# Transposing q and k of batches 2 to 7 by the DMA crossbar instead of by TensorE and VectorE, in a fused attention and feed-forward kernel

One core of a Trainium2 chip (trn2) runs the kernel. The metric is the device time of one execution in microseconds (us). PE is TensorE, DVE VectorE, ACT ScalarE, POOL GpSimd, SP SyncE.

## The reference

Attention over 8 batches, 8 heads, 576 positions, head size 64: a full attention on sums of four positions ("down", 144 of them) plus a local attention (distance under 4). The result, 4608 tokens of 512, goes through a feed-forward layer with 2048 hidden units. Cut:

```python
out_d     = sm_attn(q_d, k_d, v_d)           # q_d, k_d, v_d: means of four positions
out_up    = np.repeat(out_d, 4, axis=2)
scores    = np.where(abs(pos_i - pos_j) < 4, scale * q @ k.T, -1e9)
out_local = softmax(scores) @ v
x = (out_up + out_local)  ->  (4608, 512)
y = gelu(x @ w_in) @ w_out
```

## The kernel before

PE works through nine blocks `c` of 512 tokens. M1 (`x @ w_in`, 64 matmuls) of block c is followed by M2 (`@ w_out`, 64 matmuls), and into M2 the attention of batch c+1 is woven. From batch 2 on, PE transposes q and k of the next batch inside M1, so that scores can be taken at the start of M2. The parts that matter here:

```python
    def t_in(b, p, which):                      # one head pair, q or k
        nat = nat6(ld[b % 2]["qn" if which == "q" else "kn"])
        tr = ppool.tile([128, 1024], F16, tag="tr", name=f"tr_{which}")
        for c in range(NCK):                    # NCK = 6 pieces of CH = 96 positions
            nc.tensor.transpose(tr[:, CH * c:CH * c + CH], nat[:, c, 2 * p:2 * p + 2, :], I128[0:CH, 0:CH])
        if which == "q":
            nc.vector.tensor_copy(out=qT[:, p, :], in_=tr[:, 0:S])
            ...                                 # sums of four into qd, two adds on POOL
        else:
            for hh in range(2):                 # k goes into kz, zero-padded per head of the pair
                nc.vector.tensor_copy(out=kz[r, p, hh, :], in_=tr[r, 0:S])
            ...                                 # sums of four into kdz, on DVE

    # m2(c), at the last matmul of a 128-token tile (four to a block):
                    osb = wpool.tile([128, 512], F32, tag="osb", bufs=2, name="out_sb")
                    nc.scalar.copy(out=osb, in_=ps)
                    nc.sync.dma_start(out=out[r0:r0 + 128, :], in_=osb)

    for c in range(NCH):                        # b = c + 1
        ...
        elif b < B:
            v_down(b)                           # sums of four of v, on POOL, 5.2 us
            for p in range(NP):                 # NP = 4 head pairs
                f1(6 if p == 0 else 7)          # so many matmuls of M1
                t_in(b, p, "q")
                f1(7)
                t_in(b, p, "k")
            k_lo()
        f1()
        ...
            attn(b, f2, 6, 9, 9)                # attention among the matmuls of M2
        f2()
        if b + 1 < B:
            run(load_qk(b + 1))                 # POOL issues the loads
            run(load_v(b + 1))
```

The softmax here doesn't subtract the row's maximum and nothing guards it: scores larger than these inputs give would overflow.

## Time and profile before

| | before |
|---|---|
| time, us | 350.44 median of 3 (350.15 to 350.55) |
| span in the profile / PE busy / PE idle, us | 348.4 / 339.0 / 9.4 |
| one batch period, us | 36.22, all of it PE busy |
| DVE, ACT, POOL | 53%, 55%, 52% |

PE idle is the span less PE's busy time.

### The profile page before, as it was taken

How to read it: one execution, taken by the hardware profiler on the slowest of the kernel's cores; microseconds unless marked ns; L12 is line 12 of the kernel's file. 1: busy time of each engine (PE TensorE's matmuls, PEld its weight loads, DVE VectorE, ACT ScalarE, POOL GpSimd, SP SyncE). 2: the span in 40 equal slices, each digit the busy share in tenths (PEclk: the TensorE clock that was granted, in tenths of full speed). 3: DMA queues.
4: the chain of work that ended last, by engine and by line, in shares of the span. 5: the costliest groups of instructions: out<-in, count | busy, mean ns of one | idle time of the engine just before them, and what ended most of it. 6: DMA issues, size and time to landing. Idle time of an engine off the chain costs nothing.

```text
span 348.4 us, 7162 instructions
## 1 busy us (share of the span) xinstructions
PE 339.0 (97%) x2976; PEld 193.9 (56%) x2976; DVE 184.5 (53%) x338; ACT 192.8 (55%) x360; POOL 180.4 (52%) x243
## 2 busy tenths in 40 slices
PE   8898998999999999999999999999999999999996
PEld 4773455655665566555655575556655664444444
DVE  7793645747574857386747665676558470000000
ACT  3664465645764577357746764566556755614620
POOL 8957649633977298628963797369652000000000
PEclk9999999999999999999999999999999999999999
DMA  6999999920999099908990599129940001011002
GB/s 87 165 205 144 185 164 110 182 75 0 98 159 146 2 77 152 176 0 59 154 171 23 36 148 178 41 18 150 159 79 0 32 33 59 2 60 60 0 34 89
DMA packets 126543, 32.31 MB, mean 93 GB/s; under 512 B 109616, under 2 KB 122032, under 8 KB 126512
## 3 DMA queue, kind: packets, MB, share of 16 engines
q0 software_dynamic: 121184, 22.43, 82.2%
q1 hardware_dynamic: 5328, 9.44, 7.6%
q8 instruction: 23, 0.38, 0.4%
q14 instruction: 8, 0.07, 0.1%
HBM read 44.83 MB, written 9.44 MB: 156 GB/s over the span
## 4 chain that ended last, share of the span: by engine, by line
PE 88%; DMA 6%; DVE 2%; POOL 2%; issue 1%; ACT 0%; POOLq 0%
PE m_ps L224 35%; PE m_ps L200 33%; PE sc L348 4%; DMA w_in_sb<-in_moe_w_in_dram 3%; PE av L403 2%; PE tr_o L441 2%; DMA q_nat<-in_q_dram 2%; PE tr_k L237 2%; PE tr_q L237 2%; DMA k_nat<-in_k_dram 1%; DVE kz L272 1%; PE av L397 1%; PE sc L353 1%; PE m_ps L215 1%; PE av L395 1%; DVE kdz L275 1%
## 5 line engine op out<-in xcount | busy, mean ns | idle before, releaser
L200 PE MATMUL m_ps<-xT,w_in_sb 128*128 128x512 f16 x568 | 133.3, 379 | 0.5 <-ACT gT L195 0.5
L224 PE MATMUL m_ps<-w_out_sb,gT 128*128 128x512 f16 x560 | 130.3, 379 | 0.0
L203 ACT ACTIVATE gT<-m_ps 128x512 f16<-128x512 f32 x142 | 84.8, 597 | 56.7 <-PE m_ps L200 56.7
L200 PEld LDWEIGHTS <-w_in_sb 128*128 128x128 f16 x568 | 52.1, 97 | 54.7 <-issue 0.8
L224 PEld LDWEIGHTS <-gT 128*128 128x128 f16 x560 | 51.9, 98 | 54.6
L228 ACT COPY out_sb<-m_ps 128x512 f32<-128x512 f32 x35 | 20.6, 589 | 42.8 <-PE m_ps L224 37.8
L243 POOL TENSOR_TENSOR q_t<-qT 128x288 f32<-128x288 f16 x24 | 16.0, 667 | 52.0 <-DVE qT L240 37.8
L104 POOL DMA_DIRECT2D q_nat<-in_q_dram x42 | 32.6, 789 | 8.1 <-DMA w_out_sb<-in_moe_w_out_dram 5.7
L252 DVE TENSOR_REDUCE kdz<-kz 64x144 f16<-64x576 f16 x48 | 35.9, 747 | 1.5
L445 DVE TENSOR_TENSOR xT<-tr_o,xd 128x576 f16<-128x576 f16 x28 | 21.2, 758 | 26.9 <-ACT xd L444 26.9
L104 POOL DMA_DIRECT2D k_nat<-in_k_dram x42 | 32.2, 778 | 6.3 <-DMA w_in_sb<-in_moe_w_in_dram 3.5
L418 DVE TENSOR_TENSOR nall<-av,rr 128x896 f16<-128x896 f32 x29 | 31.7, 1091 | 1.0
L248 DVE COPY kz<-tr_k 64x576 f16<-64x576 f16 x48 | 21.9, 455 | 18.2 <-PE tr_k L237 17.5
L381 DVE TENSOR_TENSOR e<-e,band 128x1152 f16<-128x1152 f16 x28 | 21.0, 751 | 17.6 <-ACT e L375 17.6
L219 DVE COPY out_sa<-m_ps 128x256 f32<-128x256 f32 x2 | 0.8, 424 | 54.9 <-PE m_ps L215 54.9
L116 POOL DMA_DIRECT2D v_win<-in_v_dram x30 | 26.6, 912 | 0.0
L348 PE MATMUL sc<-qT,kz 128*128 128x112 f16 (+1 forms) x320 | 25.6, 214 | 0.0
L373 ACT ACTIVATE e<-sc 128x680 f16<-128x680 f32 x32 | 23.4, 732 | 2.0 <-PE sc L348 2.0
L348 PEld LDWEIGHTS <-kz 128*128 128x128 f16 x320 | 21.6, 97 | 0.9
L311 POOL TENSOR_TENSOR v_t<-v_grp 128x1024 f32<-128x1024 f16 x6 | 12.7, 2118 | 17.0 <-DMA v_grp<-in_v_dram 17.0
L444 ACT COPY xd<-tr_o 128x144 f16<-128x144 f16 x28 | 7.7, 276 | 22.0 <-PE tr_o L441 22.0
L375 ACT ACTIVATE e<-sc 128x472 f16<-128x472 f32 x32 | 18.2, 569 | 0.0
(168 smaller groups left out, 407.6 us busy)
## 6 DMA issues: line engine op xcount, KB each, us to landing
out_dram<-out_sb SPq DMA_DIRECT2D x35, 256.0 KB, 3.2
v_win<-in_v_dram POOLq DMA_DIRECT2D x40, 128.0 KB, 9.6
q_nat<-in_q_dram POOLq DMA_DIRECT2D x42, 96.0 KB, 3.7
k_nat<-in_k_dram POOLq DMA_DIRECT2D x42, 96.0 KB, 4.2
v_grp<-in_v_dram POOLq DMA_DIRECT2D x6, 512.0 KB, 8.8
w_in_sb<-in_moe_w_in_dram POOLq DMA_DIRECT2D x4, 512.0 KB, 8.1
w_out_sb<-in_moe_w_out_dram POOLq DMA_DIRECT2D x4, 512.0 KB, 9.4
v_lo<-in_v_dram POOLq DMA_DIRECT2D x6, 64.0 KB, 8.8
```

What stands on the lines that cost most here:

```text
L104: nc.gpsimd.dma_start(out=nat6(ld[b % 2][nm])[:, c, :, :], in_=src[b, :, CH * c:CH * c + CH, :].rearrange("h s d -> s h d"))
L116: nc.gpsimd.dma_start(out=L["vw"][:, j, :, 0:64], in_=v[b, :, W0[j]:W0[j] + 128, :].rearrange("h s d -> s h d"))
L200: nc.tensor.matmul(out=ps, lhsT=w_in_sb[:, fc, 128 * j:128 * j + 128], rhs=xT[:, fc, 512 * c:512 * c + 512], start=(fc == 0), stop=(fc == 3))
L203: nc.scalar.activation(out=g[:, j, :], in_=ps, func=ACTF.Gelu)
L224: nc.tensor.matmul(out=ps, lhsT=g[:, j, 128 * t:128 * t + 128], rhs=w_out_sb[:, j, :], start=(j == 0), stop=(j == NJ - 1))
L248: nc.vector.tensor_copy(out=kz[r, p, hh, :], in_=tr[r, 0:S])
L252: nc.vector.tensor_reduce(out=kdz[r, p, hh, :], in_=kz[r, p, hh, :].rearrange("p (g r) -> p g r", r=4), axis=AX.X, op=ALU.add)
L348: nc.tensor.matmul(out=dst, lhsT=kz[:, p, hh, W0[j]:W0[j] + 128], rhs=qT[:, p, Q0[j]:Q0[j] + QW[j]], start=(b > 0), stop=True)
L373: nc.scalar.activation(out=e2[:, :, 0:340], in_=sc2[:, :, 0:340], func=ACTF.Exp, scale=0.125)
L381: nc.vector.tensor_tensor(out=e2, in0=e2, in1=band.unsqueeze(1).broadcast_to([128, 2, S]), op=ALU.mult)
L418: nc.vector.tensor_tensor(out=nall.rearrange("p j a c -> p a j c"), in0=av4[:, :, :, 0:64], in1=rr.unsqueeze(3).broadcast_to([128, 2, 7, 6 ...
L445: nc.vector.tensor_tensor(out=xT[:, p, S * b:S * b + S].rearrange("p (g r) -> p g r", r=4), in0=tr[:, 0:S].rearrange("p (g r) -> p g r", r=4),
```

## The change

The intent is to free PE of 8 groups of six transposes per batch (and DVE of 12 copies), by letting SP issue twelve crossbar DMA transposes per batch. They write the operands in their final form. For that, the natural k is loaded with gaps of zeros, so that one 96x1024 transpose yields the zero-padded `kz`. The operands are double-buffered (`qTs`, `kzs`), to be filled a phase ahead; to pay for the space, the natural q and k have one buffer instead of two. ACT issues the outputs, since SP's queue now holds the transposes. The order of POOL changes: sums and v_down of batch b, then loads of batch b+1. Core of the diff:

```diff
-    qT = cpool.tile([128, NP, S], F16, tag="qT", name="qT")
+    qTs = [cpool.tile([128, NP, S], F16, tag=f"qT{i}", name="qT") for i in range(2)]
-    kz = cpool.tile([128, NP, 2, S], F16, tag="kz", name="kz")
+    kzs = [cpool.tile([128, NP, 2, S], F16, tag=f"kz{i}", name="kz") for i in range(2)]
...
+                if nm == "kn" and b > 1:           # two half pieces, with gaps of zeros
+                    for hh in range(2):
+                        nc.gpsimd.dma_start(
+                            out=pad(nat[nm])[:, c, :, 192 * hh:192 * hh + 64],
+                            in_=i.rearrange("(a g) s d -> g s a d", g=2)[hh])
...
+    def turn_qk(b):
+        for c in range(NCK):
+            cs = slice(CH * c, CH * c + CH)
+            nc.sync.dma_start_transpose(
+                out=kzs[b % 2].rearrange("p a g s -> p (a g) s")[:, :, cs],
+                in_=pad(nat["kn"])[:, c, :, :].rearrange("p a x -> p (a x)"))
+            nc.sync.dma_start_transpose(
+                out=qTs[b % 2][:, :, cs],
+                in_=nat6(nat["qn"])[:, c, :, :].rearrange("p h d -> p (h d)"))
...
-                    nc.sync.dma_start(out=out[r0:r0 + 128, :], in_=osb)
+                    nc.scalar.dma_start(out=out[r0:r0 + 128, :], in_=osb)
...
         elif b < B:
+            sums(b)                                # 4 on DVE (k), 4 x 2 on POOL (q)
+            k_lo()
             v_down(b)
-            for p in range(NP): ... t_in(b, p, "q") ... t_in(b, p, "k")
-            k_lo()
+            if b + 1 < B:
+                load_qk(b + 1)
+                turn_qk(b + 1)
+                run(load_v(b + 1))
```

More of the change, by code (lines that the diff above doesn't have):

```diff
@@ L64 @@
         ld.append({
-            "qn": ipool.tile([CH, 4096], F16, tag="qn", name="q_nat"),
-            "kn": ipool.tile([CH, 4096], F16, tag="kn", name="k_nat"),
             "vw": ipool.tile([128, 5, H, 65], F16, tag="vw", name="v_win"),
@@ L73 @@
         })
+    nat = {"qn": cpool.tile([CH, 4096], F16, tag="qn", name="q_nat"),
+           "kn": cpool.tile([CH, 6144], F16, tag="kn", name="k_nat")}
+    regr = wpool.tile([CH, 2, 4096], F16, tag="gT", bufs=2, name="regr")
     Gb = cpool.tile([128, 240], F16, tag="Gb", name="Gb")
@@ L80 @@
     zt = cpool.tile([128, 512], F16, tag="zt", name="zt")
-    e_t = [cpool.tile([128, 2 * S + 8], F16, tag=f"e{i}", name="e") for i in range(4)]
-    e_t0 = e_t
+    e_t = [cpool.tile([128, 2 * S + 8], F16, tag=f"e{i}", name="e") for i in range(3)]
     turn = [0]
@@ L97, in nat8, with pad @@
     def nat8(t):
-        return t[0:72, :].rearrange("p (h r d) -> p h r d", h=H, r=8)
+        return t[0:72, 0:4096].rearrange("p (h r d) -> p h r d", h=H, r=8)
+    def pad(t):
+        return t.rearrange("p (c a x) -> p c a x", c=NCK, a=NP)
     def load_qk(b):
-        for nm, src in (("qn", q), ("kn", k)):
-            for c in range(NCK):
-                nc.gpsimd.dma_start(
-                    out=nat6(ld[b % 2][nm])[:, c, :, :],
-                    in_=src[b, :, CH * c:CH * c + CH, :].rearrange("h s d -> s h d"))
-                yield
+        for c in range(NCK):
+            for nm, src in (("kn", k), ("qn", q)):
+                i = src[b, :, CH * c:CH * c + CH, :]
+                if nm == "kn" and b > 1:
[3 more added lines that the diff above has]
+                            in_=i.rearrange("(a g) s d -> g s a d", g=2)[hh])
+                else:
+                    nc.gpsimd.dma_start(out=nat6(nat[nm])[:, c, :, :], in_=i.rearrange("h s d -> s h d"))
+    def turn_qk(b):
+        for c in range(NCK):
+            cs = slice(CH * c, CH * c + CH)
[5 more added lines that the diff above has]
+                in_=nat6(nat["qn"])[:, c, :, :].rearrange("p h d -> p (h d)"))
     def load_v(b):
@@ L126, in load_qk8 @@
             nc.gpsimd.dma_start(
-                out=nat8(ld[b][nm])[:, h0:h1, :, :].rearrange("p h r d -> p h (r d)"),
+                out=nat8(nat[nm])[:, h0:h1, :, :].rearrange("p h r d -> p h (r d)"),
                 in_=src[b, h0:h1].rearrange("h (p r) d -> p h (r d)", r=8))
@@ L145 @@
         nc.vector.memset(ld[i]["vls"][:, 64:65], 4.0)
-    for i in range(4):
+    for i in range(3):
         nc.vector.memset(e_t[i][:, 2 * S:2 * S + 8], 1.0)
@@ L177 @@
                                     fill=0.0, base=3, channel_multiplier=4)
-    nc.vector.memset(kz.rearrange("p a b s -> p (a b s)").bitcast(F32), 0.0)
+    nc.vector.memset(kzs[0].rearrange("p a b s -> p (a b s)").bitcast(F32), 0.0)
     nc.vector.memset(KL.bitcast(F32), 0.0)
@@ L228, in m2, with sums @@
                     nc.scalar.copy(out=osb, in_=ps)
-                    nc.sync.dma_start(out=out[r0:r0 + 128, :], in_=osb)
+                    nc.scalar.dma_start(out=out[r0:r0 + 128, :], in_=osb)
                 yield
-    def t_in(b, p, which):
-        nat = nat6(ld[b % 2]["qn" if which == "q" else "kn"])
-        tr = ppool.tile([128, 1024], F16, tag="tr", name=f"tr_{which}")
-        for c in range(NCK):
-            nc.tensor.transpose(tr[:, CH * c:CH * c + CH], nat[:, c, 2 * p:2 * p + 2, :],
-                                I128[0:CH, 0:CH])
-        if which == "q":
-            nc.vector.tensor_copy(out=qT[:, p, :], in_=tr[:, 0:S])
-            qg = qT[:, p, :].rearrange("p (g r) -> p g r", r=4)
+    def sums(b):
+        for p in range(NP):
+            with nc.allow_low_precision(reason="sums of four, kept in fp16 as before"):
+                nc.vector.tensor_reduce(out=kdz[:, p, :, :],
+                                        in_=kzs[b % 2][:, p, :, :].rearrange("p a (g r) -> p a g r", r=4),
+                                        axis=AX.X, op=ALU.add)
+            qg = qTs[b % 2][:, p, :].rearrange("p (g r) -> p g r", r=4)
             t2 = wpool.tile([128, Sd, 2], F32, tag="qt2", bufs=2, name="q_t2")
@@ L244, in t_in @@
             nc.gpsimd.tensor_tensor(out=qd[:, p, :], in0=t2[:, :, 0], in1=t2[:, :, 1], op=ALU.add)
-        else:
-            for hh in range(2):
-                r = slice(64 * hh, 64 * hh + 64)
-                nc.vector.tensor_copy(out=kz[r, p, hh, :], in_=tr[r, 0:S])
-            for hh in range(2):
-                r = slice(64 * hh, 64 * hh + 64)
-                with nc.allow_low_precision(reason="sums of four, kept in fp16 as before"):
-                    nc.vector.tensor_reduce(out=kdz[r, p, hh, :],
-                                            in_=kz[r, p, hh, :].rearrange("p (g r) -> p g r", r=4),
-                                            axis=AX.X, op=ALU.add)
     def t_in_g(b, p, which):
-        nat = nat6(ld[b]["qn" if which == "q" else "kn"])
+        nt = nat6(nat["qn" if which == "q" else "kn"])
         trf = ppool.tile([128, 512], F32, tag="tr", name=f"tg_{which}")
@@ L260, in t_in_g @@
         for c in range(NCK):
-            nc.tensor.transpose(tr[:, CH * c:CH * c + CH], nat[:, c, 2 * p:2 * p + 2, :],
+            nc.tensor.transpose(tr[:, CH * c:CH * c + CH], nt[:, c, 2 * p:2 * p + 2, :],
                                 I128[0:CH, 0:CH])
         for c in range(NCK):
-            nc.tensor.matmul(out=trf[:, 288 + 24 * c:312 + 24 * c], lhsT=nat[:, c, 2 * p:2 * p + 2, :],
+            nc.tensor.matmul(out=trf[:, 288 + 24 * c:312 + 24 * c], lhsT=nt[:, c, 2 * p:2 * p + 2, :],
                              rhs=Gb[0:CH, 112:136], start=True, stop=True)
         if which == "q":
-            nc.vector.tensor_copy(out=qT[:, p, :], in_=tr[:, 0:S])
+            nc.vector.tensor_copy(out=qTs[b][:, p, :], in_=tr[:, 0:S])
             nc.vector.tensor_copy(out=qd[:, p, :], in_=trf[:, 288:432])
@@ L271, in t_in_g @@
                 r = slice(64 * hh, 64 * hh + 64)
-                nc.vector.tensor_copy(out=kz[r, p, hh, :], in_=tr[r, 0:S])
+                nc.vector.tensor_copy(out=kzs[b][r, p, hh, :], in_=tr[r, 0:S])
             for hh in range(2):
@@ L347, in local @@
                 nc.tensor.matmul(out=dst, lhsT=I128, rhs=nb[:, x:x + QW[j]], start=True, stop=False)
-            nc.tensor.matmul(out=dst, lhsT=kz[:, p, hh, W0[j]:W0[j] + 128],
-                             rhs=qT[:, p, Q0[j]:Q0[j] + QW[j]], start=(b > 0), stop=True)
+            nc.tensor.matmul(out=dst, lhsT=kzs[b % 2][:, p, hh, W0[j]:W0[j] + 128],
+                             rhs=qTs[b % 2][:, p, Q0[j]:Q0[j] + QW[j]], start=(b > 0), stop=True)
         for hh in range(2):
@@ L360, in scores_mm @@
                 local(sC[:, o + Q0[j]:o + Q0[j] + QW[j]], hh, j)
-        e = e_t[p % 3] if b else e_t0[p]
+        e = e_t[p % 3]
         ed = wpool.tile([128, 2, Sd], F16, tag="ed", bufs=4, name="ed")
@@ L537 @@
             n2 = "kn" if nm[1] == "k" else "qn"
-            dst = ld[1][n2][0:72, :].rearrange("p (r h d) -> p r h d", r=8, h=H)
+            dst = regr[0:72, int(nm[1] == "q"), :].rearrange("p (r h d) -> p r h d", r=8, h=H)
             nc.vector.tensor_copy(out=dst[:, :, 2 * p:2 * p + 2, :],
-                                  in_=nat8(L0[n2])[:, 2 * p:2 * p + 2, :, :].rearrange("p h r d -> p r h d"))
+                                  in_=nat8(nat[n2])[:, 2 * p:2 * p + 2, :, :].rearrange("p h r d -> p r h d"))
         elif nm[:2] in ("Tk", "Tq"):
             n2 = "kn" if nm[1] == "k" else "qn"
-            src = ld[1][n2][0:72, :].rearrange("p (r h d) -> p r h d", r=8, h=H)[:, :, 2 * p:2 * p + 2, :]
+            src = regr[0:72, int(nm[1] == "q"), :].rearrange("p (r h d) -> p r h d", r=8, h=H)
+            src = src[:, :, 2 * p:2 * p + 2, :]
             trf = banks(arg)[0][0]
@@ L556 @@
             if nm[1] == "Z":
-                cp(out=kz[r, p, hh, :].rearrange("p (t r) -> p t r", r=8), in_=tin["k", p][0][r])
+                cp(out=kzs[0][r, p, hh, :].rearrange("p (t r) -> p t r", r=8), in_=tin["k", p][0][r])
             else:
@@ L560 @@
         elif nm[:2] == "QT":
-            cp(out=qT[:, p, :].rearrange("p (t r) -> p t r", r=8), in_=tin["q", p][0])
+            cp(out=qTs[0][:, p, :].rearrange("p (t r) -> p t r", r=8), in_=tin["q", p][0])
         elif nm[:2] == "QD":
@@ L593 @@
             cp(out=xT[:, p, 512:576], in_=half[1][:, 0:64])
-    run(load_qk(1))
+    load_qk(1)
     for f in range(4):
@@ L598 @@
     load_vw(1)
+    nc.vector.memset(kzs[1].rearrange("p a b s -> p (a b s)").bitcast(F32), 0.0)
     nc.vector.tensor_copy(out=band[:, 0:116], in_=B0[:, 0:116])
@@ L614 @@
             k_lo()
+            nc.gpsimd.memset(pad(nat["kn"])[:, :, :, 64:192], 0.0)
+            load_qk(2)
+            turn_qk(2)
+            run(load_v(2))
         elif b < B:
+            sums(b)
+            k_lo()
             v_down(b)
-            for p in range(NP):
-                f1(6 if p == 0 else 7)
-                t_in(b, p, "q")
-                f1(7)
-                t_in(b, p, "k")
-            k_lo()
+            if b + 1 < B:
+                load_qk(b + 1)
+                turn_qk(b + 1)
+                run(load_v(b + 1))
         f1()
@@ L631 @@
         f2()
-        if b + 1 < B:
-            run(load_qk(b + 1))
-            run(load_v(b + 1))
 _INS = ['q', 'k', 'v', 'moe_w_in', 'moe_w_out']
```

## The prediction

> **What bounds the kernel now.** I read the page first, then PE's waits, then PE's timeline in a batch that repeats, then the DMA view and the POOL timeline. The page says which engine is full:
>
> ```profile
> span 348.4 us, 7162 instructions
> PE 339.0 (97%) x2976; PEld 193.9 (56%) x2976; DVE 184.5 (53%) x338; ACT 192.8 (55%) x360; POOL 180.4 (52%) x243
> ...
> PEclk9999999999999999999999999999999999999999
> DMA  6999999920999099908990599129940001011002
> ```
>
> PE is at 97%, the other compute engines near half, and the granted clock is full throughout. DMA is near full in somewhat more than half of the slices and empty between: it works in bursts, one per batch. A busy PE may still be a waiting PE, so I ask for PE's waits over the whole run:
>
> ```profile
> PE m_ps L547 <- DVE q_nat L539: 1.5, 1, 1.5
> PE spin L490 <- DVE dum L136: 1.3, 1, 1.3
> PE av L395 <- DVE v_lm L289: 0.8, 1, 0.8
> PE tg_k L261 <- DMA k_nat<-in_k_dram: 0.6, 2, 0.4
> ...
> PE av L397 <- DVE v_lm L291: 0.2, 1, 0.2
> ```
>
> These are all the large ones, and all lie before 57 us. From 73 us on PE never waits: batches 2 to 7 repeat with a period of 36.22 us (the first scores of batches start at 198.13 and 234.35), and in those 36.22 us PE is busy for 36.22. So PE's own instruction stream sets the end, and an instruction taken off PE there is worth exactly the slot that it occupies. The slot is read from PE's timeline:
>
> ```profile
> 180.96 1.46 PE L200 MATMUL m_ps<-xT,w_in_sb 128*128 128x512 f16 x6
> 182.25 0.42 PE L237 MATMUL tr_q<-I,q_nat 96*128 96x96 f16 x6
> 182.51 1.68 PE L200 MATMUL m_ps<-xT,w_in_sb 128*128 128x512 f16 x7
> 184.02 0.42 PE L237 MATMUL tr_k<-I,k_nat 96*128 96x96 f16 x6
> 184.28 1.68 PE L200 MATMUL m_ps<-xT,w_in_sb 128*128 128x512 f16 x7
> ```
>
> Durations overlap, so starts are to be read: six transposes hold PE from 182.25 to 182.51, 0.26 us, though one is listed with 206 ns.
>
> **What the Trainium skill says.** (1) "VectorE: DVE Perf Modes", section "The three transpose paths", gives 390 ns for a 128x128 two-byte transpose on TensorE and 1309 ns for the DMA crossbar. This trace does not agree for PE: in a stream one 96x96 piece costs 0.26/6 = 43 ns. So little is to be won per transpose, and the crossbar must win by being elsewhere, not by being quick. (2) "DMA: Bandwidth & Descriptors", section "Latency and other measured facts", gives 261 GB/s for a DMA transpose in one kernel. No run yet shows it here. (3) The same page, "Issuing engines are not separate DMA queues": DMAs of all engines run on the same 16 DMA engines and interleave. The trace cannot contradict it: outputs (SP) and loads (POOL) never need the whole. (4) "TensorE: Matmul & The Clock Gate", section "What's actually happening": after about 3.4 us of idleness PE runs at half clock until busy for as long again. The trace has no such gap after the start; the change could make one.
>
> **The change, part by part.**
>
> *Off PE.* Per batch 2 (q, k) x 4 (head pairs) groups of six transposes: 8 x 0.26 = 2.07 us; six batches: 12.4 us. Cross-check: the first matmul phase with transposes lasts from 180.96 to 196.84, 15.88 us; the last one, without, from 289.77 to 303.58, 13.81; the difference is 2.07, times 6 is 12.4. Nothing of it is hidden, since PE is the full engine. The new period would be 34.15 us.
>
> *Off and onto VectorE.* It loses the copies (4 of 0.46 and 8 of 0.46, 5.5 us a batch) and does the sums of four as 4 whole ones in place of 8 halves of 747 ns (6.0 us). A half has 576 inputs; one of 1152, counted as twice, is at most 1.5 us, so about 6 us. DVE falls from 23.2 us of 36.2 to under 18 of 34: no gain in time, it was not the bound.
>
> *Onto ScalarE.* The 28 outputs of the batches are now issued by ACT, 332 ns each on SP today: about 1.3 us per period for an engine busy 21.9 of 36.2. Free by itself. What each issue waits for is not (rival 1).
>
> *POOL.* k is loaded in 12 half pieces instead of 6. A 768-row issue takes 0.78 us and v_lo, of 128 rows, 0.62, so a half is about 0.70 by interpolation: 12 x 0.70 - 6 x 0.78 = +3.7 us; POOL goes from 24.6 of 36.2 to about 28.3 of 34.15. Fits.
>
> *DMA.* Two views of before:
>
> ```profile
> DMA  9773000000000000599999999999999999994600
> ...
> q0 software_dynamic: 17114, 2.58, 86.0%
> q1 hardware_dynamic: 864, 1.57, 10.4%
> ...
> v_win<-in_v_dram POOLq DMA_DIRECT2D x5, 128.0 KB, 9.3
> q_nat<-in_q_dram POOLq DMA_DIRECT2D x6, 96.0 KB, 3.7
> ```
>
> This is the stretch 180 to 222 us, in slices of 1.05 us: the loads of one batch and its outputs keep the DMA engines going for about 23 slices, 24 us, because the rows are small (128 bytes landed), not because there are many bytes. The change adds, per batch, 6 transposes of 96x1024 and 6 of 96x512 two-byte elements (half of k's is zeros): 1.77 MB. At the skill's 261 GB/s that is an estimate of 6.8 us. 24 + 7 = 31 us of DMA in a period of 34: it fits, with 3 us to spare.
>
> *The loop across batches.* POOL does the sums for q (4 x 1.1 us), v_down (5.2 us: 213.12 to 218.5), 18 loads (13 us), v's loads (6 us), then needs the next transposes. That is 28 to 31 us against 34.15, so transposes are ready before they are due, and the double buffer lets them be a phase early. DVE and POOL sums then run at the end of the previous period; the scores that need them come 15 us into the next.
>
> **The rivals.**
>
> *Rival 1: a new wait on ACT, once.* The instruction order of the changed kernel lists each wait. The first output of batch 0's tokens, now in ACT's own stream, waits for the eighth crossbar transpose of batch 2, only because hardware DMAs share eight completion semaphores. Batch 2's loads can no longer run ahead: q and k have one natural buffer, and POOL first waits for PE's last k transposes of batch 1 (45.5 us) and clears the padding (an estimate of 3 us: 3072 elements at the 1 ns of its 512-element select of 0.61 us). The eighth transpose's data are issued by 46 + 3 + 8 = 57 us, land 4 us later, and the transpose takes about 3 (an output's landing time): 64 us. ACT reaches its output at 58.3 and stalls until 64. PE runs on until 62.3, where the output transposes want the PSUM tile that ACT frees; then the exponentials are late too. I make it 4 us lost, once; between 0 and 8, more if the transposes are slow or PE's clock drops. In later batches the first such wait is for the fifth transpose of the next batch, due about 13 us into the period against the output's 19.5: no loss. For it: the wait is in the program. Against: nothing but its size is open.
>
> *Rival 2: DMA becomes the bound.* If the crossbar took not 7 but 15 us per batch, the DMA sum is 39 us, the period follows it, and 6 x (39 - 36.2) makes 367. At 1309 ns for each of the 72 128-wide blocks, one after another, it would be 94 us a batch and some 700 us in all. For it: small rows already fill 24 us. Against: 1309 ns is less than any DMA of this trace takes to land, so it is a latency, and 16 engines work side by side.
>
> *Rival 3: hidden anyway.* If PE's transposes had filled gaps, the time would stay at 350. Against it: no PE wait in the batches.
>
> **Range and chances.** 350.4 - 12.4 + 4 = 342.0 us. Without rival 1's loss it is 338, with twice its loss 346; a slightly DMA-bound loop gives 345 to 355. Faster by 2% means under 343.4, and my centre lies close to it: 57% faster. A larger stall or a period held at 35 to 37 us by DMA: 29% the same. A slow crossbar: 14% slower. Range 337 to 354.
>
> **What would show it.** Right: PE's groups of tr_q and tr_k gone; period about 34.15 us and PE without waits from 90 us on; a PE wait of some 4 us between 58 and 70 us whose chain leads through ACT's output issue to a transpose; DMA active about 31 us of each period; kernel time 342. Wrong: a period above 34.5, with PE waiting for kdz, qd or an exponential; transposes taking over 3 us each from issue to landing; ACT stalls at outputs in later batches; a PE clock below full after 60 us.

## The result

The changed kernel takes **387.41 us** (median of 4 runs, 383.16 to 392.18) against 350.50 in the same rounds. It is slower: the ratio is 1.097, with a 95% interval from 1.091 to 1.103. All ratios here are the mean of one kernel's fast runs over the mean of the other's fast runs of the same rounds, so not quite the ratio of the medians quoted. Two of the four runs, and with them the profiled one (389.21), count as slow, being over 1.5% above the fastest. The times of a run that stalls vary more; the fast two, 385.62 and 383.16, carry the verdict, and the profile is read for its mechanism (the profiles of e2 and e4 below are of fast runs and show waits of the same kind).

Lines of the page of the changed kernel:

```profile
span 387.5 us, 6727 instructions
...
PE 342.8 (88%) x2688; PEld 189.8 (49%) x2688; DVE 148.2 (38%) x242; ACT 192.3 (50%) x360; POOL 203.5 (53%) x280
...
PEclk9999999999968999599979998799969999999999
DMA  7999999990999999993999199959998001002002
```

PE runs 288 instructions fewer, and yet is busy for 3.8 us more. The clock row says why: it is no longer 9 throughout. DMA, which came in bursts, is now busy in most slices up to slice 31. PE idles for 387.5 - 342.8 = 44.7 us, 35 more than before.

One period costs as follows (windows from one M1 phase to the next; start:end, length, then PE busy first; PEclk, DMA share and GB/s last):

```profile
212.48:253.49 41.01, 36.62 (x282) 20.43 (x280) 16.81 (x24) 21.83 (x41) 28.68 (x40) 0.92 1.41 130
253.49:294.42 40.93, 36.64 (x281) 20.49 (x280) 17.66 (x24) 21.84 (x41) 29.09 (x41) 0.92 1.29 136
294.42:328.68 34.26, 34.26 (x281) 19.01 (x280) 16.68 (x23) 21.83 (x41) 6.64 (x9) 1.00 0.08 32
```

The last of these windows has no next batch to load and transpose. It takes 34.26 us, all of it PE: what the prediction promised (34.15). The other two take 41: 4.3 us more of idle PE, and 2.4 us of PE time stretched by a lower clock (36.62 against 34.26 for the same instructions). The earlier periods were longer: 47.0, 44.1 and 41.5 us from one start of M1 to the next. PE's largest wait of the whole run (who, for whom: us in all, times, longest), and then one of these waits, in the chain that ended last, in order of time (start, us, what):

```profile
PE tr_o L444 <- DVE nall L424: 34.8, 6, 9.7
```

```profile
228.36 1.94 PE m_ps L242 x9
...
232.59 6.07 DMA qT<-q_nat
...
238.73 0.35 ACTq L247
...
239.18 0.29 ACT xd L450
...
239.49 0.76 DVE xT L451
...
240.44 1.10 DVE nall L424
...
241.59 0.29 PE tr_o L444
```

Read it upwards from PE. An output transpose of the attention (tr_o) waits for a normalized head pair (nall). DVE makes that only after xT, which needs ACT's copy xd. ACT was held at line 247, the issue of an output. That output reads nothing but out_sb; what released it is a crossbar transpose of q, of the *next* batch. ACT's timeline shows the hole:

```profile
232.60 0.60 ACT L246 COPY out_sb<-m_ps 128x512 f32<-128x512 f32 x1
238.73 0.35 ACTq L247 DMA_DIRECT2D out_dram<-out_sb  x1
239.18 0.28 ACT L450 COPY xd<-tr_o 128x144 f16<-128x144 f16 x1 [5.98 <-DMA qT<-q_nat]
```

The data are in out_sb at 233.2; the issue starts at 238.73. A completion semaphore is the counter on which a DMA reports that it has landed. In the trace's records, the DMAs issued by SP and ACT report on the same eight semaphores (numbers 111 to 118). This output and the sixth transpose of the next batch both have number 115; that transpose was issued at 232.59 and landed at 238.66, just before the output was issued. Each of PE's 6 waits, 34.8 us in all, follows an output that was held in this way.

There is a second finding in the same period. POOL starts the sums of a batch at 211.47 and those of the next at 251.79:

```profile
211.47 0.66 POOL L259 TENSOR_TENSOR q_t<-qT 128x288 f32<-128x288 f16 x1 [11.65 <-PE tr_o L447]
...
251.79 0.66 POOL L259 TENSOR_TENSOR q_t<-qT 128x288 f32<-128x288 f16 x1 [11.37 <-issue]
```

The releasers in the brackets are inferred, and here they mislead: by the trace's landing times, the last transposes land at 211.26 and 251.57, 0.2 us before the sums start, and the sums read what they write. So there is a loop of 40.3 us: sums 4.5, v_down 5.3, loads of q and k 13.2 (221.3 to 234.5), then 11.0 until SP has issued the last transpose (245.5) and 6.2 until it has landed and the sums start. All five turns of this loop take 39.8 to 41.8 us, and PE's periods come down to 41. SP's own timeline of one batch's twelve transposes runs from 224.78 to 245.5; these are its first, third last and last two:

```profile
224.78 1.21 SPq L120 DMA_TRANSPOSE kz<-k_nat  x1
...
238.37 1.94 SPq L123 DMA_TRANSPOSE qT<-q_nat  x1
240.41 3.49 SPq L120 DMA_TRANSPOSE kz<-k_nat  x1
243.99 1.53 SPq L123 DMA_TRANSPOSE qT<-q_nat  x1
```

The DMA view of the period from 212.48 to 253.49, in slices of 1.03 us:

```profile
DMA  9610000000999999999999999998999999999999
...
q1 hardware_dynamic: 7296, 1.77, 32.7%
```

The engines rest for some 8 us, while POOL makes sums and v_down, and are full for the 30 slices after; in all about 32 us of 41. The second line is the transposes' own (packets, MB, share of the 16 engines' time).

So three theories stand against each other. **A**: ACT's waits on semaphores shared with the transposes. **B**: the loop through POOL, SP and the crossbar, longer than PE's 34.2 us of work. **C**: the DMA engines have too much to do in a period.

### The profile page after: what moved, and what is told of

It reads as the page before. It is cut to its first block, busy times and chain, and to the rows that moved or that the text cites. A ratio compares the mean times of both kernels' runs of the same rounds, so it can differ in the third digit from the quotient of the medians.

```text
span 387.5 us, 6727 instructions
## 1 busy us (share of the span) xinstructions
PE 342.8 (88%) x2688; PEld 189.8 (49%) x2688; DVE 148.2 (38%) x242; ACT 192.3 (50%) x360; POOL 203.5 (53%) x280
## 4 chain that ended last, share of the span: by engine, by line
PE 61%; DMA 22%; POOL 9%; DVE 3%; ACT 2%; issue 1%; SPq 1%; ACTq 0%; POOLq 0%
PE m_ps L242 24%; PE m_ps L218 24%; DMA qT<-q_nat 8%; DMA v_win<-in_v_dram 6%; PE sc L354 3%; PE av L409 2%; DMA out_dram<-out_sb 2%; DMA w_out_sb<-in_moe_w_out_dram 2%; PE tr_o L447 2%; DMA k_nat<-in_k_dram 2%; DVE nall L424 1%; DMA q_nat<-in_q_dram 1%; DMA kz<-k_nat 1%; POOL k_nat L111 1%; POOL v_t L317 1%
## 5 line engine op out<-in xcount | busy, mean ns | idle before, releaser
L242 PE MATMUL m_ps<-w_out_sb,gT 128*128 128x512 f16 x560 | 136.8, 393 | 0.0
L218 PE MATMUL m_ps<-xT,w_in_sb 128*128 128x512 f16 x568 | 126.5, 379 | 0.8 <-ACT gT L213 0.5
L221 ACT ACTIVATE gT<-m_ps 128x512 f16<-128x512 f32 x142 | 84.8, 597 | 44.8 <-PE m_ps L218 43.4
L218 PEld LDWEIGHTS <-w_in_sb 128*128 128x128 f16 x568 | 54.8, 98 | 67.4 <-issue 3.3
L242 PEld LDWEIGHTS <-gT 128*128 128x128 f16 x560 | 53.9, 101 | 59.3 <-issue 8.5
L111 POOL DMA_DIRECT2D k_nat<-in_k_dram x72 | 49.7, 703 | 2.9 <-DMA q_nat<-in_q_dram 1.8
L444 PE MATMUL tr_o<-I,nall 128*128 128x128 f16 x28 | 6.5, 234 | 34.8 <-DVE nall L424 34.8
L254 DVE TENSOR_REDUCE kdz<-kz 128x288 f16<-128x1152 f16 x24 | 30.7, 1344 | 7.4 <-DMA kz<-k_nat 7.4
L354 PE MATMUL sc<-qT,kz 128*128 128x112 f16 (+1 forms) x320 | 28.3, 228 | 0.0
L354 PEld LDWEIGHTS <-kz 128*128 128x128 f16 x320 | 24.0, 106 | 0.9
L444 PEld LDWEIGHTS <-nall 128*128 128x128 f16 x28 | 2.8, 99 | 41.1 <-DVE nall L424 38.9
```

The source lines that it names most:

```text
L111: nc.gpsimd.dma_start(out=pad(nat[nm])[:, c, :, 192 * hh:192 * hh + 64], in_=i.rearrange("(a g) s d -> g s a d", g=2)[hh])
L218: nc.tensor.matmul(out=ps, lhsT=w_in_sb[:, fc, 128 * j:128 * j + 128], rhs=xT[:, fc, 512 * c:512 * c + 512], start=(fc == 0), stop=(fc == 3))
L221: nc.scalar.activation(out=g[:, j, :], in_=ps, func=ACTF.Gelu)
L242: nc.tensor.matmul(out=ps, lhsT=g[:, j, 128 * t:128 * t + 128], rhs=w_out_sb[:, j, :], start=(j == 0), stop=(j == NJ - 1))
L254: nc.vector.tensor_reduce(out=kdz[:, p, :, :], in_=kzs[b % 2][:, p, :, :].rearrange("p a (g r) -> p a g r", r=4), axis=AX.X, op=ALU.add)
L354: nc.tensor.matmul(out=dst, lhsT=kzs[b % 2][:, p, hh, W0[j]:W0[j] + 128], rhs=qTs[b % 2][:, p, Q0[j]:Q0[j] + QW[j]], start=(b > 0), stop=True)
```

## The experiments

All kernels were compared with the reference and found right within its tolerance. That says little about q and k: e1, whose q and k are not transposed at all, passes as well, probably because the reference draws q and k as 0.1 times normal numbers, so that scores are near zero and the weights nearly uniform. So no run proves that the transposed operands are right. Line numbers differ between kernels; names don't.

| run | POOL's order | output issued by | k | us | ratio to before | PE idle |
|---|---|---|---|---|---|---|
| changed kernel | sums first | ACT, 4 a block | padded | 387.41 | 1.097 | 44.7 |
| e2 | sums first | ACT, 1 a block | padded | 375.58 | 1.068 | 36.4 |
| e11 | sums first | SP, 1 a block | padded | 372.78 | 1.060 | 32.6 |
| e3 | loads first | ACT, 4 a block | padded | 382.31 | 1.064 | 45.1 |
| e6 | loads first | ACT, 1 a block | padded | 364.31 | 1.038 | 31.2 |
| e10 | loads first | SP, 1 a block | padded | 358.12 | 1.019 | 23.4 |
| e7 | sums first | ACT, 4 a block | unpadded | 391.34 | 1.116 | 49.1 |
| e8 | loads first | ACT, 1 a block | unpadded | 357.18 | 1.019 | 26.4 |
| e9 | loads first | SP, 1 a block | unpadded | 344.27 | 0.979 | 14.0 |
| e1 | no transposes | ACT, 4 a block | padded | 340.74 | 0.968 | 9.7 |

PE idle is span less PE busy, of the profiled run. The medians of the changed kernel and of e3 take in slow runs, and their profiled runs are slow ones; so runs are compared by the ratio, which takes fast runs alone.

### e1: no transposes at all

```diff
     def turn_qk(b):
-        for c in range(NCK):
+        for c in range(0):
```

(and a memset of one operand that would else be unwritten; wrong q and k.)

> All 72 crossbar transposes left out, loads, sums, outputs and PE's stream as in the changed kernel (wrong result on purpose: the operands keep their zeros or old data). If the transposes and what waits for them are the whole loss, the time is 350.5 - 12.4 = 338 us, at most 341, with a period of 34.2 us and PE's clock full. Rival: the split loads and the later start of POOL alone slow the batches: then 345 us or more.

Measured: 340.74 us, ratio 0.968 (0.965 to 0.972), periods of 34.26 us from 107 us on, full clock. So the transposes and all that waits for them cost some 45 us; everything else in the change (padded loads, ACT's outputs, POOL's order, single natural buffers) costs at most some 1.5 us, since 10.9 of the 12.4 us are gained against the 351.65 of these rounds. In the repeated batches the saving on PE is as predicted. What is left to find is what makes the transposes dear.

### e2: one output per block

```diff
-                    nc.scalar.dma_start(out=out[r0:r0 + 128, :], in_=osb)
+                    if t == 3:      # osb is [128, 4, 512] and holds the whole block
+                        nc.scalar.dma_start(
+                            out=out[512 * c:512 * c + 512, :].rearrange("(a p) d -> p a d", p=128), in_=osb)
```

(The last block keeps single outputs, for a short tail. The block's buffer is single, and the dummy operand `zt` moves into xT to make room. All this holds for e6 and e8 to e12 too.)

> The four outputs of a batch's token block go out in one DMA at its end, still from ACT (buffer of four parts); the transposes are untouched. Theory A, ACT's wait on a completion semaphore shared with the next batch's transposes is the whole loss: 338 to 343 us. Theory B, the loop sums, v_down, loads, 12 transposes, landing takes 40.3 us whatever ACT does: the slack of some 14 us before the scores need the sums is used up first, then the period is again near 40: about 370 us, with PE waiting for kdz or qd instead of for what ACT frees.

Measured: 375.58 us, 1.068. The waits in the middle of M2 are gone, and two things remain. ACT still waits for a transpose at the block's one output, and now holds up the first Gelu of M1. And DVE and POOL wait for the transposed operands, as theory B has it. Waits (engine, line, for whom: us in all, times, longest):

```profile
PE m_ps L218 <- ACT gT L221: 22.6, 5, 10.5
...
DVE kdz L257 <- DMA kz<-k_nat: 42.3, 6, 11.1
```

POOL's sums start at 204.14 and 243.91: a loop of 39.8 us. The experiment doesn't separate A from B, since removing three of four outputs did not remove A.

### e3: loads first

```diff
+            if b + 1 < B:
+                load_qk(b + 1)
+                turn_qk(b + 1)
             sums(b)
             k_lo()
             v_down(b)
             if b + 1 < B:
-                load_qk(b + 1)
-                turn_qk(b + 1)
                 run(load_v(b + 1))
```

This takes sums and v_down, 9.8 us, out of the loop of theory B.

> On POOL the loads of the next q and k stand ahead of the sums and v_down (9.8 us), all else as in the changed kernel, ACT's shared wait too. Theory B: the loop loses 9.8 of its 40.3 us, so it is 30.5, under PE's 34.2; the transposes land early enough for ACT too: about 343 us. Rival C, the DMA engines are full (they were busy 30 of 41 us): the order does not matter, over 375 us. Theory A alone makes no claim on the loop; it also expects a gain, since the awaited transpose lands earlier.

Measured: 382.31 us (372.48 to 388.87, 5 runs; fast ones 372 to 376), 1.064. The profiled run, 388.55, is one of the slow ones. A clear miss of the 343 us. The transposes now wait for their operand buffer, which the attention of the block just before still reads (SP waits 44.6 us for PE's attention instructions), and come in a different phase. ACT's shared wait moved with them to the third and fourth outputs:

```profile
PE m_ps L218 <- ACT gT L221: 23.3, 4, 11.0
PE m_ps L218 <- DVE xT L451: 7.9, 5, 5.4
```

The edit did not cure B as meant either. The loads of q and k now stand in POOL's queue right behind the loads of v of the batch before, and in the trace's records POOL's loads report on eight semaphores of their own (103 to 110), so they wait for those loads of v to land (on number 105, for example, a load of v landed at 216.33 and the next load of k was issued at 216.62):

```profile
POOL k_nat L111 <- DMA v_win<-in_v_dram: 22.1, 16, 3.8
```

In the changed kernel this wait was 0.3 us. From 214.74 to 239.29 POOL takes 24.6 us to issue one batch's loads of q and k, against 13.2. So with A in place, this order of POOL gives a part only: the ratio goes from 1.097 to 1.064.

### e4: half as many, larger transposes

q and k of a piece share one natural tile and one operand tile, and one 96x1536 transpose does what one of 96x1024 and one of 96x512 did.

```diff
-            nc.sync.dma_start_transpose(out=kzs[...][:, :, cs], in_=pad(nat["kn"])[:, c, ...])
-            nc.sync.dma_start_transpose(out=qTs[...][:, :, cs], in_=nat6(nat["qn"])[:, c, ...])
+            nc.sync.dma_start_transpose(out=kqs[b % 2][:, :, cs], in_=natt[:, 1536 * c:1536 * c + 1536])
```

> q and k of one chunk in one 96x1536 transpose: 6 per batch in place of 12, the same bytes. If a transpose costs SP its 1.3 us per instruction whatever its size (as k's and q's in the changed kernel suggest), the chain of transposes shrinks from 20.7 us to the 13 us of POOL's load issue and the loop from 40.3 to about 33; also the outputs no longer share a semaphore with late transposes: 340 to 350 us. If the cost goes with the bytes (2 x 1.3 or more per instruction): the loop stays near 40: 368 us or more.

Measured: 388.44 us, 1.105; no gain. The duration of SP's instruction (minimum, median, maximum in ns) and the landing time (us) of the 36 transposes:

```profile
L127 SPq DMA_TRANSPOSE kq<-kq_nat x36: 1247/2279/7370, 57.2 to 289.3; - x36
...
DMA to landing us min/median/max: 5.1/9.3/14.0
```

The minimum stays at 1.25 us, but the median rises to 2.28 and the maximum to 7.37. What holds SP then isn't shown; e5, next, has short issues where there is little other traffic. So SP's count of issues is not the limit by itself.

### e5: the transposes alone, in a quiet stretch

e1, with twelve transposes of dead data in the last block, where no loads run: six small ones each waiting for the one before, then six free ones of 96x1024.

```diff
+        if c == NCH - 1:
+            for cols, rows in ((1024, 96), (512, 96), (128, 96), (1024, 16), (1024, 96), (512, 96)):
+                nc.sync.dma_start_transpose(out=kk[:, 0:cols // 128, 0:rows], in_=src[0:rows, 0:cols])
+            for i in range(6):
+                nc.sync.dma_start_transpose(out=k1[:, :, CH * i:CH * i + CH], in_=src[:, 1024 * i:1024 * i + 1024])
```

> As the run without transposes, but in the last, load-free token block SP issues transposes of dead data: first six of different sizes, each made to wait for the one before by writing the same place (96x1024, 96x512, 96x128, 16x1024, 96x1024, 96x512), then six of 96x1024 free to overlap. If a transpose is slow by itself: 5 us or more from issue to landing with quiet DMA engines, and the free six take 10 us or more. If it was slow only beside the loads: about 3 us each, SP busy 1.2 us per instruction whatever the size, the free six landed within 9 us, which is 6 x 1.2 plus a landing.[...]

Measured (one run, of unknown state, 338.64 us): SP takes 1.12 to 1.33 us for each of the serial six whatever their size, and they land after 2.3 to 4.4 us, median 2.6. The free six are issued one after another:

```profile
269.04 8.58 SPq L643 DMA_TRANSPOSE kz<-k_nat  x6
```

That is 1.4 us each; they land after 2.9 to 4.7 us. The last is issued at 276.4 and lands at 279.3, so the six take 10.3 us from first issue to last landing. That is over the 9 us that were expected of a quick transpose, but by SP's issues one after another, not by a slow landing. In the changed kernel the same 96x1024 transposes take 4.3 to 10.8 us, median 6.7:

```profile
L120 SPq DMA_TRANSPOSE kz<-k_nat x36: 1212/1306/3522, 56.0 to 280.3; - x36
...
DMA to landing us min/median/max: 4.3/6.7/10.8
```

So a transpose lands in about 3 us by itself; beside the loads its landing takes twice as long.

### e6: loads first and one output (e2 and e3 together)

> Loads ahead of sums and v_down, and one output DMA per token block: ACT's shared wait comes only at the block's end and the loop is 30.5 us by its own steps. Theory B (the loop and the shared wait are all): 343 us or less. Theory C (what the DMA engines have to do per batch is near 40 us, so no order helps): 368 us or more, period near 39, DMA busy in nearly every slice of the batches.

Measured: 364.31 us, 1.038. PE's waits of some size have shrunk to one line:

```profile
PE m_ps L218 <- ACT gT L221: 19.6, 3, 10.8
```

Three times, the block's one output waits for a transpose (11.3 us for one of q, 9.7 for those of k); between them the periods are 34.3 us. Theory C's strong form, that a period can't be shorter than some 40 us because of DMA, is refuted by those periods.

### e7: k unpadded

```diff
-    kzs = [... [128, NP, 2, S] ...  for i in range(2)]
+    kTs = [cpool.tile([128, NP, S], F16, tag=f"kT{i}", name="kT") for i in range(2)]
+    kzs = [cpool.tile([128, NP, 2, S], F16, tag="kz", name="kz")] * 2
...
+        for hh in range(2):      # DVE puts the halves into the padded operand, as before the change
+            nc.vector.tensor_copy(out=kzs[0][r, :, hh, :], in_=kTs[b % 2][r, :, :])
```

k is loaded in 6 pieces instead of 12 halves, and all transposes are 96x512: a third fewer bytes through the crossbar.

> k is transposed without zeros, 96x512 like q, into its own double buffer; VectorE copies it into the one padded operand (two copies per batch) and sums from it. Transposed bytes fall by a third (1.77 to 1.18 MB a batch), load issues from 18 to 12 per batch; ACT's shared wait and POOL's order as in the changed kernel. Theory B: the loop loses some 4 us of issue: 387 falls to about 365. Theory C: the DMA work falls by a third of the transposes' share: also about 365; if transposes cost by the instruction only (12 as before): 380 or more.

Measured: 391.34 us, 1.116; a miss. ACT waited for the transposes of k for 36.4 us in 5 places. The loop hardly changed: POOL issued the loads of a batch in 9.9 us instead of 13.2, yet its turns took 37.4 to 44.8 us. Less DMA work is worth nothing as long as A and B stand.

### e8: unpadded k, loads first, one output (e6 and e7 together)

> The unpadded k with both other edits (loads first, one output). If transposed bytes and the two waits are the whole loss: period 34.3 and 340 to 343 us, which would beat the kernel before by 2 to 3%. If DMA work still exceeds 34 us per batch: 350 to 360.

Measured: 357.18 us, 1.019. One wait of PE is left:

```profile
PE m_ps L213 <- ACT gT L216: 16.7, 1, 16.7
```

An output whose copy is done at 73.13 us is issued only at 89.79, when a transpose of the next batch has landed: semaphore sharing again. All later periods are 34.3 us.

### e9, e10, e11: the output issued by SP

The last step of A: SP issues the one output per block. Then no ACT instruction of a batch should wait for a transpose; in the traces of e9, e10 and e11 no wait of ACT is ended by a DMA.

```diff
-                        nc.scalar.dma_start(
+                        nc.sync.dma_start(
                             out=out[512 * c:512 * c + 512, :].rearrange("(a p) d -> p a d", p=128), in_=osb)
```

e9 is e8 with this, e10 is e6 with this, e11 is e2 with this. e11 thus has B alone, e10 neither A nor B.

> Unpadded transposed k, loads and transposes first, and the output of a token block in one DMA that SyncE issues, so that no ScalarE instruction of a batch waits for a transpose. Theory A (ScalarE's wait on a completion semaphore shared with the next batch's transposes decides): the single 16.7 us stall of e8 is gone, 340 to 342 us, 3% faster than the kernel before, periods of 34.3 us. Theory B or C (the loop through GpSimd and SyncE, or full DMA engines, decide): 350 us or more, with TensorE waiting for the operands q and k of the next batch.

> The same with the padded operands of the change. Theory A: e6 less the 19.6 us that TensorE waited for ScalarE there, 343 to 346 us. Theory C (the padded transposes' work fills the DMA engines): 355 us or more, with waits for q and k.

> The change with one thing moved: the output of a token block in one DMA, issued by SyncE; GpSimd's order as in the change. Theory A alone: 341 to 346 us. Theory B (sums, v_down, loads, transposes and their landing are a loop of 40 us, longer than a batch's 34.3): 365 to 372 us, with TensorE or VectorE waiting for the transposed q and k at the start of each batch's scores and none for ScalarE.

Measured: e11 **372.78 us** (1.060, 1.056 to 1.064); e10 **358.12** (1.019, 1.014 to 1.023); e9 **344.27** (0.979, 0.975 to 0.982, 6 runs).

**e11 shows B by itself.** PE never waits for ACT in a batch, but the chain in order of time leaves PE in the M1 phase and runs through the loop:

```profile
229.16 0.88 PE m_ps L218 x4
...
233.92 8.99 DMA qT<-q_nat
...
243.09 0.66 POOL q_t L262
...
247.64 2.61 POOL v_t L320
...
250.31 1.27 POOL v_d L321
...
252.44 1.07 POOL v_lm L325
...
254.64 3.33 PE m_ps L242 x9
```

The last transpose lands at 242.9, the sums and v_down follow on POOL, and PE, which needs v_d and v_lm for the attention, waits for them (5 times each, 20.1 us in all). M1 phases start at 148.5, 189.4, 229.0 and 270.9: periods of 39.6 to 41.9 us. The expectation named q and k as what is waited for; that holds for DVE (its sums wait 65.5 us for the transposes of k). For PE it is POOL's v_down, next in the queue behind the sums of q, that comes last.

**e9 shows that, after its first period, neither A nor B nor C is left.** Windows of e9:

```profile
72.90:112.94 40.04, 35.71 (x281) 19.72 (x280) 21.11 (x29) 22.03 (x41) 31.90 (x42) 0.96 1.96 155
112.94:147.08 34.14, 34.14 (x281) 19.03 (x280) 19.72 (x30) 21.93 (x41) 25.36 (x33) 1.00 1.88 140
```

From 112.94 us on, every period is 34.14 us and all of it PE. Against the kernel before e9 is about 2% faster; whether by more than 2% is unclear, since the interval reaches from 1.8 to 2.5%. It falls 3.5 us short of e1 because of its first period: POOL's sums of batch 2 start only at 85.64 us, behind the loads of batch 3 in its queue (issued from 65.44 us on, with waits for loads of v as in e3), and PE waits for v_d and v_lm (2.6 and 1.7 us) and loses clock.

**e10 against e9** is worth 14 us, 358.12 against 344.27, and differs in the padding alone, with what goes with it (in e9 DVE copies k into the padded operand): 12 loads of k instead of 6 (POOL's issues of k take 48.9 us instead of 33.3) and a half more bytes through the crossbar. e10 loses in its first period, which takes 50.0 us and in which PE waits 8.3 us for POOL's sum of q, and once later (36.1 us). Which of the two, POOL's issues or the bytes, does it was not separated.

### e12: sums first in batch 2 alone

```diff
-            if b + 1 < B:
+            if b > 2 and b + 1 < B:
                 load_qk(b + 1)
                 turn_qk(b + 1)
             sums(b)
             k_lo()
             v_down(b)
+            if b == 2:
+                load_qk(3)
+                turn_qk(3)
```

> e9 with one thing changed: in batch 2 alone GpSimd makes the sums and v_down before it issues the loads of batch 3. In e9 these sums began at 85.64 us, after batch 2's own transposes had long landed, and batch 2 took 40.0 us against 34.1 of the others. If GpSimd's order is the cause: batch 2 takes 34 to 36 us and the time is 339 to 341 us. If the late loads of batch 3 then hold up batch 3 by as much (they come after v_down, so its transposes are due some 45 us after batch 2 began): 343 to 346 us, as e9, with the lost time in batch 3.

Measured: 349.79 us, 0.996; worse than e9. Batch 2 does take 34.18 us, but batch 3 pays for it with 45.43:

```profile
72.50:106.68 34.18, 34.18 (x281) 19.05 (x280) 18.97 (x28) 21.92 (x41) 25.86 (x33) 1.00 1.26 114
106.68:152.11 45.43, 38.78 (x282) 21.02 (x281) 19.89 (x30) 22.14 (x41) 32.70 (x42) 0.89 1.91 151
```

Batch 3's transposes are issued up to 109.3 us and have landed by 115.5, but the sums begin only at 124.56. The loads of batch 4 stand ahead of them on POOL, from 104.85 us on, and POOL idles for 10.1 us among them until loads of v, issued just before, have landed. The second alternative of the expectation was right in kind and too mild: 11 us are lost in batch 3, against 5.9 in batch 2 of e9. One late turn of the loop was moved and grew.

## Why the prediction was wrong

**What held.** The value of PE's transposes: 12.4 us, period 34.15. It was 34.26 in the window without transposes and in e1 from 107 us on, and 34.14 in e9 from 112.94 us on. PE's groups of transposes are gone. DVE's wide sum took 1344 ns (predicted at most 1.5 us), the clearing of the padding 2.65 us (predicted 3). DMA's work: about 32 us of the period were busy, 31 were predicted, and e6, e8 and e9 had periods of 34.1 to 34.4 us, so it fits. (The agreement of the sum is in part luck: the transposes' packets took 32.7% of 41 us, 13.4 us, where the prediction had 6.8; loads and transposes overlap.) The mechanism of rival 1, ACT's output waiting for a transpose over a shared semaphore, was named. Its size came out by luck: PE's first wait, at 71 us, was 4.8 us, 4 were predicted. But by the semaphore records the first output did not wait for the eighth transpose of batch 2. It waited for the first, and was held by 1.3 us; it was the second output that was held by 5.0 us, by the sixth transpose.

**What failed, first: "In later batches the first such wait is for the fifth transpose of the next batch, due about 13 us into the period against the output's 19.5: no loss."** The transposes come later than that. In the period from 212.48, the first was issued 12.3 us in. ACT had its output ready 20.7 us in, and the transpose that held it (the sixth in SP's order) was issued 20.1 us in and landed 26.2 us in. So the wait came back batch after batch, 6 PE waits with 34.8 us in all, where the prediction counted 4 us once. The lower clock after such stalls, of which the prediction's fourth point from the skill had warned, came with it: with each of the 6 waits the granted clock was 0.50 for 3.4 to 10.2 us (for example from 239.41 to 246.24), which makes 0.92 on average in a period with 4.3 us of idleness. The output's time was right within 1.2 us; the transpose's was off by 13 us, twice the margin of 6.5 that the prediction thought it had.

**What failed, second: "That is 28 to 31 us against 34.15, so transposes are ready before they are due."** The sum had the right terms up to the last load: sums 4.4 (measured 4.5), v_down 5.2 (5.3), loads 13 (13.2). It ended there, with v's loads, which are not even in the loop, in place of what follows: SP works off its twelve transposes for 11.0 us after the last load is issued, and the last lands 6.2 us later. The sum is 40.2, measured 40.3. Two sizes were missing. SP's own time, 1.2 to 1.3 us for each transpose and up to 3.5 under load, appeared in no part of the working. And "the transpose takes about 3 (an output's landing time)" was right for a quiet chip (e5: median 2.6 to 3.4) and wrong for the place where it was used: 6.7 beside loads. The first failure hangs on this second one: the transposes of a period come late because the turn of the loop before ended late.

**How the two share the loss.** Neither is "the" cause; each alone leaves most of it. By the ratio to the kernel before, the change is at 1.097. With A removed and B left (e11) it is 1.060; with POOL's order changed and A left (e3), 1.064; with both, 1.019 (e10), and with the padding gone as well, 0.979 (e9). Curing only the padding (e7, 1.116) gave nothing. Between the changed kernel and e1, the profiled spans differ by 387.5 - 337.8 = 49.7 us: 35.0 are PE idle, and 14.7 are PE busy (342.8 - 328.1), the same instructions, or nearly, at a lower clock. The prediction mentioned a lower clock and put no figure on it; it is 30% of the loss. (This is the split of a slow run; the two fast runs had granted clocks of 0.951 and 0.955 on average.)

**Of the rivals**, 2 (DMA as the bound) was wrong in its simple form; what was true of it is that the transposes land later beside loads. Its slowest form, 1309 ns for each 128-wide block one after another, is refuted by e5, where 48 such blocks took 10.3 us. Rival 3, hidden anyway, is refuted by e1.

**Range and chances.** 342.0 with a range to 354 left no room for 387. A slower outcome was given 14%, for a slow crossbar; by itself the crossbar was not slow (e5), but its transposes came late.

## What to carry to other kernels

Work that moves from the full engine to a DMA is free only if the loop that feeds it fits in a period: add up, along one turn of the loop, the queue in which the loads stand, the issuing engine's own time per transfer, and the landing time *under the load of that place*. Before moving a DMA issue to a compute engine, look up in the compiled instruction list what it waits for: a completion semaphore shared with someone else's transfers makes that engine wait for them. And cure such causes together: here no repair alone brought the ratio from 1.097 below 1.060, two (e4, e7) were worth nothing, and together they brought it to 0.979. That is also why a single repair that fails doesn't refute its theory.

## What the Trainium skill lacked or had wrong

- "VectorE: DVE Perf Modes", "The three transpose paths": its 390 ns for a 128x128 transpose on TensorE is far from the slot that a 96x96 one occupies in a stream of others (43 ns; the removal of 288 of them was worth 12.4 us of PE time). Its 1309 ns for the crossbar was not seen as a time to landing: the shortest was 2.3 us, in the quiet stretch of e5, the median beside loads 6.7 us. (No transpose of 128x128 was run.)
- "DMA: Bandwidth & Descriptors": the bandwidth it gives for a DMA transpose (261 GB/s) led to an estimate of 7 us per batch; the transposes' packets took 13.4 us of the 16 engines' time in a period. What decided was not bandwidth: SP is taken for 1.1 to 1.3 us by each transpose, about the same for 96x128, 96x512, 96x1024 and 96x1536, and up to 7.4 us when the DMA engines are loaded (e4). The landing time depends as much on the neighbours: median 2.6 to 3.4 us alone, 6.7 beside loads. The page has no landing time of a transpose; for the issuing engine's time it has only cycle counts of unnamed "previous generations", in a table on trn3.
- No page tells that DMAs issued by SP and by ACT can share completion semaphores, so that an issue on ACT waits for an unrelated transpose of SP (and POOL's loads for POOL's earlier loads). Here PE waited 34.8 us in 6 waits behind such issues; with the output issued by SP, PE had no such wait.
